# Reordering the head, halving the GpSimd casts and redrawing the instruction lists of a fused sliding-window attention and GEGLU kernel

## The chip, the core and the metric

One core of one Trainium2 chip. The metric is device microseconds of one launch. A profile shows one execution; its span is shorter than the time of the same run (341.0 against 342.76 us before), so spans are compared with spans and times with times. A ratio is the mean time of one kernel's fast runs over that of the other's fast runs of the same rounds, so it is not quite the ratio of the medians quoted.

In the profile PE is TensorE's matmuls, PEld its weight loads, DVE is VectorE, ACT is ScalarE, POOL is GpSimd, SP is SyncE. L581 is line 581 of the kernel; in kernels with halved GpSimd instructions line numbers are 4 higher (L464 is L468, L581 is L585, L427 is L431, L521 is L525).

## The reference

```python
# q, k, v: 8 batches x 8 heads x 576 positions x 64; windows of 32, for heads 4 to 7 dilated by 4
scores = scale * q @ k^T
mask_plain = (rel >= 0) & (rel < 32)
mask_dil   = (rel >= 0) & (rel < 128) & (rel % 4 == 0)
attn = softmax(where(mask, scores, -1e9));  x = attn @ v          # x as 4608 tokens x 512
out = (gelu(x @ w_gate) * (x @ w_val)) @ w_out                    # 512 -> 1536 -> 512
```

## The kernel before

The feed-forward part runs in 8 chunks of 512 tokens. A chunk has a gate stage (192 matmuls of 512 columns, whose results ScalarE puts through gelu and VectorE multiplies) and an output stage (48 matmuls). The attention of later batches is woven between these matmuls, so that TensorE never waits. Where each unit stands is written down in lists of places, one string per stage. A number takes so many feed-forward matmuls; `S` is a pair of heads' score products, `P` the exponential on ScalarE, `M` the mask multiply on VectorE, `D` and `N` the denominators and the products with v, `T` and `B` the reciprocal of the denominators by two VectorE transposes (or `A`, the same by ScalarE), `X` the final product that writes the feed-forward input `xT`. `g` and `u` are the gelu and the product of a gate block, `e` an output copy, `G` and `E` table loads.

```python
    def run_program(c, words, mms, banks):        # walks one list; every engine's instructions are written in this order
        ...
    gates = { ...
        3: ("G 6 e3@2 2 g0 3 u0 2 g1 4 u1 4 g2 ...
    outs = { ...
        3: ("1 u11 5 S16@0 1 E P16 10 e0@3 1 M16 1 S17@0 1 P17 D16@0 N16@1 T16 2 S18@0 M17 ...
```

The head of the program, and what GpSimd does after it:

```python
    warm(20, 7)                                   # 20 matmuls on ones; the granted clock is full from 5.46 us on
    for t in views(1)[2:]:                        # k and v of batch 1: 8 clears (memsets to zero) on VectorE
        zero(t, nc.vector)
    nc.vector.tensor_reduce(class_of, ident..., op=ALU.max)
    biases()                                      # the masks as a bias for batch 0's scores
    for t, hp, eng in ((0, 0, "dve"), (0, 1, "act"), (1, 0, "dve"), (1, 1, "pool")):
        cast_six(eng, t, hp)                      # first q and k rows, fp32 to fp16
    load_w(0); bias_first(0, 4); bias_first(1, 6)
    ...
    def second():
        for t in views(2)[2:4]: zero(t)           # GpSimd
        load_w(2)
        ...                                       # q, k of batch 1, w_out
        for t in views(2)[4:]: zero(t)
        two_masks()
        for t in blocks(vraw[0], 1), blocks(vraw[0], 0): zero(t)
        ...
```

For each later batch, q, k and v come by DMA in fp32, GpSimd casts them to fp16, a DMA transposes q and k, and GpSimd spreads k into block diagonals:

```python
    def cast_plain(t, i):                         # one instruction of 128x1280
        nc.gpsimd.tensor_copy(s16[:, 1280*t : 1280*t+1280]..., st_of(i)...)
    def cast_v(dst, i):                           # two of 64x1152
        for x in range(2): nc.gpsimd.tensor_copy(dst[half, :, half], st[half])
    def spread_plain(kp):                         # two of 64x1152
        for x in range(2): spread(nc.gpsimd, kp..., kdp[:, :, 0:S]..., x)
```

The softmax here doesn't subtract the row's maximum and nothing guards it: scores larger than these inputs give would overflow.

## Time and profile before

| | before |
|---|---|
| median of 4 runs beside the changed kernel | 341.94 us (341.58 to 342.97) |
| span of the profiled run | 341.0 us |
| TensorE, VectorE, ScalarE, GpSimd busy | 97%, 50%, 44%, 40% |
| first score product, first gate matmul | 12.03 us, 21.41 us |
| holes of TensorE after 25 us | 2.23 us in 7 places |

TensorE is the bound, so the question is only where it does not work. "Hole" here is the distance between the starts of two neighbouring matmuls, less what the first one's columns take (216 ns for 512, in proportion for fewer), from the trace's start times. Only holes over 0.11 us are counted, which leaves out the changes between transposes and matmuls of some 0.1 us each. The lines of this profile stand in the prediction.

### The profile page before, as it was taken

To read this page: it belongs to the slowest core of one execution; us is meant where nothing else is said; L and a number is where in the kernel's file an instruction comes from. 1 tells how busy PE (TensorE), PEld (TensorE's weight loads), DVE (VectorE), ACT (ScalarE), POOL (GpSimd) and SP (SyncE) were. 2 spreads that over 40 slices of the span, in tenths; PEclk is the share of its full clock that TensorE was granted. 3 is DMA by queue.
4 is the path that set the end of the run, shared out by engine and by line. 5 is a ranking of instruction groups with operands and counts; after the bars stand their busy time and mean duration, and the time that the engine had idled before them with its cause. 6 is when DMAs were issued, how large, how long until landed. Compare 5 with 4: busy or idle time off the path is not lost.

```text
span 341.0 us, 6228 instructions
## 1 busy us (share of the span) xinstructions
PE 331.2 (97%) x2404; PEld 169.4 (50%) x2404; DVE 171.1 (50%) x265; ACT 150.7 (44%) x222; POOL 135.8 (40%) x194
## 2 busy tenths in 40 slices
PE   7879999999999999999999999999999999999996
PEld 3744456444644465445554465446544544444443
DVE  7864454533843465335983389446833423303320
ACT  2653456635553457335623553346434353223321
POOL 8697777475407556556626701492000000000000
PEclk9999999999999999999999999999999999999999
DMA  7999977997749699898689517981100110020002
GB/s 183 198 194 198 199 164 167 261 188 186 237 117 187 164 222 170 226 232 188 203 209 196 146 63 187 233 191 68 64 0 2 62 63 1 0 94 31 0 31 94
DMA packets 108957, 47.89 MB, mean 140 GB/s; under 512 B 83584, under 2 KB 104448, under 8 KB 108928
## 3 DMA queue, kind: packets, MB, share of 16 engines
q1 hardware_dynamic: 97200, 39.99, 48.3%
q0 software_dynamic: 11184, 6.79, 14.2%
q10 hardware_dynamic: 544, 0.72, 0.8%
q8 instruction: 19, 0.31, 0.4%
q14 instruction: 10, 0.08, 0.1%
HBM read 37.75 MB, written 9.44 MB: 138 GB/s over the span
## 4 chain that ended last, share of the span: by engine, by line
PE 88%; DVE 8%; issue 2%; POOL 1%; ACT 0%; DVEq 0%; ACTq 0%
PE ps L581 54%; PE ps L588 23%; PE ps L523 5%; PE ps L427 3%; DVE xT L573 1%; DVE P L464 1%; DVE dt L543 1%; PE ps L362 1%; DVE rb L560 1%; PE ps L612 1%; DVE v L196 1%; DVE q L196 1%; POOL q L261 1%; DVE dense L345 1%; DVE bias L131 0%
## 5 line engine op out<-in xcount | busy, mean ns | idle before, releaser
L733 DVE SCALAR_TENSOR_TENSOR u_all<-g,ps 128x512 f16<-128x512 f16 x108 | 73.9, 685 | 107.9 <-PE ps L581 100.7
L728 ACT ACTIVATE g<-ps 128x512 f16<-128x512 f32 x108 | 64.3, 597 | 114.1 <-PE ps L581 114.1
L581 PE MATMUL ps<-xT,wg 128*128 128x512 f16 x432 | 112.6, 379 | 0.2
L581 PE MATMUL ps<-xT,wv 128*128 128x512 f16 x432 | 112.5, 379 | 0.0
L588 PE MATMUL ps<-wo,u_all 128*128 128x512 f16 x420 | 101.5, 379 | 0.0
L581 PEld LDWEIGHTS <-wg 128*128 128x128 f16 x432 | 42.1, 98 | 50.3
L581 PEld LDWEIGHTS <-wv 128*128 128x128 f16 x432 | 41.9, 98 | 50.2 <-issue 0.9
L588 PEld LDWEIGHTS <-u_all 128*128 128x128 f16 x420 | 37.5, 97 | 36.8
L261 POOL COPY q<-dense 64x512 f16<-64x512 f16 (+2 forms) x56 | 36.4, 677 | 25.6 <-DMA dense<-s 22.9
L459 ACT ACTIVATE P<-ps 128x832 f16<-128x832 f32 (+1 forms) x32 | 26.7, 836 | 21.9 <-PE ps L427 21.2
L250 POOL CAST v<-stage 64x1152 f16<-64x1152 f32 x28 | 33.0, 1179 | 4.4 <-DMA stage<-in_v_dram 3.4
L599 ACT ACTIVATE osb<-ps 128x512 f32<-128x512 f32 x34 | 20.3, 596 | 32.1 <-PE ps L588 31.6
L573 DVE TENSOR_TENSOR xT<-ps,rb 128x576 f16<-128x576 f32 x32 | 29.6, 928 | 9.4 <-ACT rb L554 4.7
L210 POOL CAST s<-stage 128x1280 f16<-128x1280 f32 x12 | 15.4, 1280 | 46.9 <-DMA stage<-in_q_dram 32.5
L543 DVE STREAM_TRANSPOSE dt<-ps 128x576 f32<-128x576 f32 x21 | 16.3, 774 | 14.5 <-PE ps L523 14.3
L222 POOL CAST s<-stage 128x512 f16<-128x512 f32 x24 | 14.4, 631 | 10.7 <-DMA stage<-in_q_dram 9.0
L523 PEld LDWEIGHTS <-two_ones 128*128 128x128 f16 x176 | 13.5, 97 | 8.3 <-issue 1.7
L523 PE MATMUL ps<-P,two_ones 128*128 128x64 f16 (+8 forms) x176 | 16.2, 226 | 0.8 <-DVE P L464 0.6
L523 PEld LDWEIGHTS <-v 128*128 128x128 f16 x280 | 13.8, 98 | 5.4 <-issue 1.0
L560 DVE STREAM_TRANSPOSE rb<-rc 128x576 f32<-128x576 f32 x21 | 16.2, 769 | 0.2
L464 DVE TENSOR_TENSOR P<-P,two_d 128x768 f16<-128x768 f16 x14 | 10.6, 759 | 9.4 <-ACT P L459 9.4
L427 PEld LDWEIGHTS <-q 128*128 128x128 f16 x252 | 13.0, 98 | 4.5 <-POOL q L261 0.2
(72 smaller groups left out, 174.9 us busy)
## 6 DMA issues: line engine op xcount, KB each, us to landing
out_dram<-osb SPq DMA_DIRECT2D x35, 256.0 KB, 2.2
stage<-in_v_dram SPq DMA_DIRECT2D x32, 144.0 KB, 3.7
stage<-in_v_dram SPq DMA_DIRECT2D x28, 128.0 KB, 3.1
stage<-in_q_dram SPq DMA_DIRECT2D x24, 128.0 KB, 3.0
stage<-in_k_dram SPq DMA_DIRECT2D x24, 128.0 KB, 3.0
stage<-in_q_dram SPq DMA_DIRECT2D x6, 512.0 KB, 5.0
stage<-in_k_dram SPq DMA_DIRECT2D x6, 512.0 KB, 5.8
wg<-in_moe_w_gate_dram POOLq DMA_DIRECT2D x6, 256.0 KB, 6.8
```

The source lines that it names most:

```text
L250: nc.gpsimd.tensor_copy(dst[half, :, half], st[half])
L261: eng.tensor_copy(dst[half, :, :, half], src[half])
L427: nc.tensor.matmul(o, lhs, rhs, start=st, stop=True, skip_group_check=True)
L459: nc.scalar.activation(pt[:, 0 : src.shape[1]], src, AF.Exp, bias=0.0, scale=scale)
L523: nc.tensor.matmul(o, lhs, rhs, start=st, stop=True, skip_group_check=True)
L543: nc.vector.transpose(dt.rearrange("p b c -> p (b c)"), psf[:, c0 : c0 + S])
L573: nc.vector.tensor_tensor(dst, num, rb, ALU.mult)
L581: nc.tensor.matmul(ps[:, bank, :], w[:, kc, ns], xT[kc][:, tok], start=first, stop=end)
L588: nc.tensor.matmul(ps[:, bank, :], u_all[:, fc, tb * P : (tb + 1) * P], wo_t[fc // 4][:, fc % 4, :], start=(fc == 0), stop=(fc == NNB - 1),)
L599: nc.scalar.activation(osb, ps[:, bank, :], AF.Copy, bias=0.0, scale=1.0 / USCALE)
L728: nc.scalar.activation(g, ps[:, gate_banks(c, args[0])[0], :], AF.Gelu)
L733: nc.vector.scalar_tensor_tensor(u_all[:, nb, :], tiles.pop(("g", nb)), USCALE, val, ALU.mult, ALU.mult)
```

## The change

The intent: VectorE makes the bias masks before most of its clears, so that the first casts wait for data alone; GpSimd's long instructions are halved, so that a mask multiply that meets one is held up for less time (the one at 87.80 us took 1.55 us beside a cast of 1.25 us, one of the same shape at 124.03 us 0.49); the lists are drawn up anew with longer VectorE durations, so that a late VectorE instruction does not stop TensorE. With the lists go two smaller edits: the last columns of k (`rest` in the diff) are copied from PSUM on VectorE or ScalarE, for the later batches instead of by GpSimd from a copy, and the order of the first gate matmuls changes. The core of the diff (cut marks are dots):

```diff
     def cast_plain(t, i):
-        nc.gpsimd.tensor_copy(... "p (g k c) -> p k g c" ...)
+        for g in range(2):
+            nc.gpsimd.tensor_copy(s16[:, 1280 * t + 640 * g : 1280 * t + 640 * g + 640]..., st_of(i)...[:, :, g])
...  (cast_v and spread_plain in the same way, two halves by g)
-            copy("pool" if b else "dve", rest, kdd[:, hp, :, P:NCL]...)
+            copy(("dve", "act")[eng], rest, col.rearrange("p (r i) -> p i r", r=8)[:, 64:R8, :])
...
-    for t in views(1)[2:]:
-        zero(t, nc.vector)
     nc.vector.tensor_reduce(class_of, ...)
+    zero(views(1)[2], nc.vector)
     biases()
+    zero(views(1)[3], nc.vector)
...
     def second():
-        for t in views(2)[2:4]:
+        load_w(2)
+        for t in views(1)[4:] + views(2)[2:4]:
             zero(t)
-        load_w(2)
...
         3: (   # gate stage of chunk 3
-            "G 6 e3@2 2 g0 3 u0 2 g1 4 u1 ...
+            "2 e3@2 X15 2 G 6 g0 3 u0 g1 4 u1 ...
         4: (
-            "G 3 T20 1 N20@1 e3@3 2 B20 g0 3 X20 3 u0 1 g1 1 D21@0 N21@1 T21 ...
+            "3 X18 N19@1 e3@3 3 G 1 X19 4 D20@0 1 T20 1 g0 N20@1 2 g1 1 u0 2 u1 3 B20 ...
...  (all lists of gates 1 to 7 and outs 0 to 6 are new, and the order of kc at the start of gates 1 to 4)
```

## The prediction

> **What bounds the kernel now.** I read the page's busy table first, then the waits of TensorE, then the chain that ended last in order of time, then the timelines of the first 25 us and of the stretches where TensorE waits.
>
> The busy table, then TensorE's groups in the page, then the answer on whom TensorE waited for over the whole span:
>
> ```profile
> PE 331.2 (97%) x2404; PEld 169.4 (50%) x2404; DVE 171.1 (50%) x265; ACT 150.7 (44%) x222; POOL 135.8 (40%) x194
> ...
> L581 PE MATMUL ps<-xT,wg 128*128 128x512 f16 x432 | 112.6, 379 | 0.2
> ```
> ```profile
> PE ps L521 <- issue: 1.6, 1, 1.6
> PE ps L628 <- DVE ones L66: 1.5, 1, 1.5
> PE ps L359 <- DVE s L345: 0.9, 1, 0.9
> PE ps L523 <- DVE P L464: 0.6, 1, 0.6
> ...
> PE ps L406 <- DVE bias L141: 0.5, 1, 0.5
> PE ps L521 <- DVE dt L543: 0.4, 1, 0.4
> ```
>
> TensorE is the bound: it is busy 97% of 341.0 us, and the span's other 3% is in the first 25 us and a few short waits. A single matmul is shown as 379 ns, but in the long runs 96 of them take 20.72 us (243.30 to 264.02 in the chain), which is 216 ns from start to start. The row therefore hides any hole shorter than about 160 ns, so I also compared the distance between the starts of neighbouring matmuls with 216 ns (or its share for narrower ones). After 25 us that leaves some 0.7 us that is merely eight changes between transposes and matmuls, and 2.3 us that is waiting: 0.26 at 50.4, 0.76 at 88.4, and 0.07, 0.13, 0.30, 0.12, 0.36, 0.30 between 130 and 171. That 2.3 us and the head are all that a reordering can win; the work of TensorE itself does not change (the order listing has the same 2404 matmuls).
>
> The head, from the timelines of VectorE and TensorE:
>
> ```profile
> 7.25 0.54 DVE L196 MEMSET v<- 64x576 f32 x1 [0.16 <-issue]
> 7.82 0.29 DVE L653 TENSOR_REDUCE class_of<-ident 128x4 f16<-128x128 f16 x1
> ...
> 8.42 1.09 DVE L131 TENSOR_TENSOR bias<-late_of,class_of 64x64 f16<-64x64 f16 x2
> ...
> 9.64 1.02 DVE L345 CAST s<-u_all 96x768 f16<-96x768 f32 x2
> ```
> ```profile
> 8.44 0.87 PE L406 MATMUL ps<-bias,ident 128*128 128x480 f16 x6 [0.50 <-DVE bias L141]
> 10.24 1.19 PE L359 MATMUL ps<-ident,s 96*128 96x96 f16 x24 [0.94 <-DVE s L345]
> ...
> 18.60 0.22 PE L521 MATMUL ps<-P,v 64*64 64x32 f16 x3 [1.62 <-issue]
> ```
>
> Eight clears, 0.70 us from start to start, keep VectorE until 7.8 us; then the bias masks take 1.9 us, and only then come the two casts, though the q rows had landed at 7.56 us and the k rows at 8.32. TensorE's first real work starts at 10.24.
>
> The worst later wait, in VectorE's and GpSimd's timelines:
>
> ```profile
> 87.80 1.55 DVE L464 TENSOR_TENSOR P<-P,two_d 128x768 f16<-128x768 f16 x1
> ```
> ```profile
> 87.69 1.25 POOL L210 CAST s<-stage 128x1280 f16<-128x1280 f32 x1 [2.08 <-DMA stage<-in_k_dram]
> ```
>
> The same mask multiply takes 0.49 us at 124.03. Here it ends at 89.35, which is 0.41 us after GpSimd's cast ends at 88.94: it stood still while that cast ran.
>
> [...] The 28 mask multiplies take 19.3 us together; at the undisturbed 0.49 and 0.53 us (two_d, two_p) they would take 14.3, so about 5 us goes to such blocking. [...] 19 packets of 16 KB in the instruction queue. The first starts at 16.38 and takes 0.96 us, and TensorE stands from 16.98 to 18.60 with nothing released; I read this as a late block. [...] what splitting costs on GpSimd I take from this trace alone.
>
> **The change, part by part.**
>
> 1. Head of VectorE. Four v clears go to GpSimd (4 x 0.70 = 2.8 us), two go behind the bias masks. Then: small clears until 2.3, class_of, two clears to 4.1; the masks then have GpSimd's band (4.07) and late_of (ends 4.34) and take 1.9 us, to about 6.0; two more clears to 7.4. The casts now wait for data: q at 7.56 to 8.1, k at 8.32 to 8.9. TensorE: warm-up to about 7.9, bias products without their 0.50 wait to 8.6, transposes of q at once, of k after ScalarE's and GpSimd's casts (GpSimd's ends at 9.20), done at about 9.6 instead of 11.3. That is 1.7 us, but not all of it stays: the next transposes read the dilated q rows, which land at 10.16 either way. They started at 11.40 and can start at 10.2: **1.2 us** is left. I expect TensorE's first score products at 10.7 to 10.9 instead of 12.03.
>
> 2. Does the block of instructions swallow that? [...] TensorE reaches the gap earlier still, so the stand is longer, but it ends at about 17.4 instead of 18.60. The chain behind it (5.8 us to the steady run at 24.4) has the same instructions. Gain kept: **1.2 us**, between 0.3 and 1.8.
>
> 3. Loads on GpSimd. The third weight load is issued before the clears (from 19.5, not 21.9), the clears grow from 4 to 8 (+2.4 us), so the q and k loads of batch 1 are issued at 27.3 rather than 24.8. The weights ahead of them land only by 32.5, so the DMA queue doesn't run dry; the six q rows still land near 33.6, five us before use. **0.**
>
> 4. Halves on GpSimd. 12 casts of 128x1280, 14 spreads and 28 v casts of 64x1152 become twice as many. Spacing of copies is 1.17 us for 1152 columns and about 0.59 for 512, so 0.13 is fixed: 54 x 0.13 = 7 us more on an engine that is 40% busy, about 1 us per batch, where spreads end 3 us or more before use except for batch 1. For it: its score products move one matmul later, and the end-columns now come from PSUM on VectorE, so two GpSimd copies (1.0 us) and their 1.4 us of waits go; I work out a margin of 0.5 us for the scores and 1 us for its first v product. The longest block on VectorE falls from 1.25 to about 0.7 us. **This alone is worth perhaps 0.5 us**, of the hole at 88.4.
>
> 5. The new lists. One denominator goes from two VectorE transposes to ScalarE; mask multiplies and final products are later relative to their inputs; in batches 4 to 7 parts of the attention move from the output stage into the gate stage. Between 158 and 171 us the chain is nearly all VectorE (its busy time is 9.93 of 10 us from 160 to 170), costing 1.1 us of holes; the new list moves the normalisation of pairs 19 to 21 past it. In the gate stage a u product may be 1.7 us late before TensorE minds (8 matmuls of 216 ns against 0.69), and one transpose (0.77) or product (up to 1.13) between two of them fits. I expect 0.8 of the 2.3 us of holes to stay or come back elsewhere. Parts 4 and 5 together: **1.5 us**.
>
> Sum: 342.15 - 1.2 - 1.5 = **339.4 us**.
>
> **The rivals.**
> (a) The head is hidden by data: weights or the instruction block set the start of the steady run. For it: the DMA queue is full; the block cost 1.6 us. Against: first weights land at 18.44, gates start at 21.4. Then only 1.5 is won: 340.7.
> (b) New waits of TensorE[...]: a v product of batch 1 nine matmuls earlier, or deferred normalisation crowding the u products. For it: VectorE is already at 80 to 100% in stretches. Against: GpSimd has margins and the lists were drawn with longer VectorE times. It would cost 1 to 3 us: 341 to 342.5.
> (c) Everything works and the head also shortens behind the block: up to 1.7 + 2.0 us, 338.0 or a little lower.
>
> **Range and chances.** The sum is 339.4; (c) gives 338.0, (a) with some of (b) 341.1. I give 338.0 to 341.1. Runs before spread 341.72 to 342.97, about 0.4%. Faster by over 2% needs 335.3, beyond all that can be won; slower by over 2% needs 6.8 us of new waits. Chances: 0.01 faster, 0.97 within, 0.02 slower.
>
> **What would show it.** Part 1: casts on VectorE at 7.6 and 8.4, first scores near 10.8. Part 2: the stand of TensorE without a releaser ends near 17.4 and the steady run starts near 23.2; if it still ends at 18.6, (a) holds. Part 3: the weights land by 32.5 as before. Part 4: no mask multiply above about 1.2 us, and spreads of 64x576 at about 0.65. Part 5: no hole over 0.3 us between 158 and 171, and TensorE's waits after 25 us under 1 us. What would make it wrong: a wait of TensorE on GpSimd's spreads or v casts at 44 to 56 us, or on xT at the starts of gate stages.

## The result

| | before | changed |
|---|---|---|
| median | 341.94 us (4 runs) | 339.26 us (4 runs, 338.70 to 339.65) |
| ratio, 95% interval | | 0.9916 (0.9888 to 0.9943) |
| span of the profiled run | 341.0 us | 337.0 us |
| first score product, first gate matmul | 12.03, 21.41 us | 11.10, 19.57 us |
| stand of TensorE in the first v products | 1.80 us, until 18.60 | 0.89 us, until 16.75 |
| holes of TensorE after 25 us | 2.23 us | 0.40 us |
| longest mask multiply | 1.55 us | 1.09 us |

The changed kernel is 0.8% faster; 339.4 had been predicted. The two profiles differ by 4.0 us of span, more than the medians, because the profiled run of before was one of its slower runs and that of the changed kernel its fastest.

The busy table and the whole answer on TensorE's waits, changed kernel:

```profile
PE 330.5 (98%) x2404; PEld 169.4 (50%) x2404; DVE 166.2 (49%) x260; ACT 150.5 (45%) x223; POOL 145.8 (43%) x250
```
```profile
PE ps L632 <- DVE ones L66: 1.5, 1, 1.5
PE ps L525 <- issue: 0.7, 1, 0.7
PE ps L525 <- DVE dt L547: 0.4, 1, 0.4
PE ps L431 <- POOL q L263: 0.2, 1, 0.2
PE ps L431 <- DVE dense L349: 0.2, 1, 0.2
```

The same 2404 matmuls. The waits on the casts (`DVE s`), the bias and the mask multiply (`DVE P`) are gone; the wait without a releaser has fallen from 1.6 to 0.7 us; a new one on GpSimd's spread has come, 0.2 us. The mask multiplies of the changed kernel (minimum, median and longest in ns), and TensorE's timeline at the new wait:

```profile
L468 DVE TENSOR_TENSOR P<-P,two_p x14: 527/606/1086, 45.5 to 234.8; 128x832 f16<-128x832 f16 x14
L468 DVE TENSOR_TENSOR P<-P,two_d x14: 494/558/1026, 50.2 to 237.1; 128x768 f16<-128x768 f16 x14
```
```profile
43.96 0.54 PE L431 MATMUL ps<-q 128*128 128x96 f16 x9 [0.24 <-POOL q L263]
```

The head, from the timelines of VectorE and TensorE of the changed kernel (start, duration, instruction, idle time before it and its releaser):

```profile
4.13 0.47 DVE L141 TENSOR_SCALAR bias<-band 64x96 f16<-64x96 f16 x2 [0.37 <-POOL band L115]
...
7.69 0.61 DVE L349 CAST s<-u_all 96x768 f16<-96x768 f32 x1 [1.10 <-DMA u_all<-in_q_dram]
8.55 0.56 DVE L349 CAST s<-u_all 96x768 f16<-96x768 f32 x1 [0.25 <-DMA u_all<-in_k_dram]
```
```profile
9.32 1.19 PE L363 MATMUL ps<-ident,s 96*128 96x96 f16 x24
...
11.10 0.56 PE L431 MATMUL ps<-q,dense 64*64 64x96 f16 x18 [0.18 <-DVE dense L349]
...
16.75 0.22 PE L525 MATMUL ps<-P,v 64*64 64x32 f16 x3 [0.71 <-issue]
```

The casts, which stood behind clears and masks until 9.64 us, now wait for the DMAs (releaser `DMA u_all`).

### The profile page after: what moved, and what is told of

It is laid out like the page before. It is cut to its first block, busy times and chain, and to the rows that moved or that the text cites.

```text
span 337.0 us, 6263 instructions
## 1 busy us (share of the span) xinstructions
PE 330.5 (98%) x2404; PEld 169.4 (50%) x2404; DVE 166.2 (49%) x260; ACT 150.5 (45%) x223; POOL 145.8 (43%) x250
## 4 chain that ended last, share of the span: by engine, by line
PE 86%; POOL 8%; DMA 4%; SPq 1%; issue 1%; DVE 0%; POOLq 0%
PE ps L585 49%; PE ps L592 27%; PE ps L527 6%; PE ps L431 3%; DMA u_all<-in_q_dram 2%; POOL v L196 2%; DMA stage<-in_v_dram 2%; POOL wv L151 1%; POOL wg L151 1%; PE ps L616 1%; POOL wo L154 1%; POOL q L196 1%; SPq L235 1%; POOL q L263 1%; POOL two_p L327 0%
## 5 line engine op out<-in xcount | busy, mean ns | idle before, releaser
L585 PE MATMUL ps<-xT,wg 128*128 128x512 f16 x432 | 114.4, 379 | 0.1
L592 PE MATMUL ps<-wo,u_all 128*128 128x512 f16 x420 | 100.2, 379 | 0.0
L585 PEld LDWEIGHTS <-wg 128*128 128x128 f16 x432 | 41.3, 98 | 47.3
L263 POOL COPY q<-dense 64x576 f16<-64x576 f16 (+2 forms) x70 | 38.3, 580 | 22.4 <-DMA dense<-s 18.7
L252 POOL CAST v<-stage 64x576 f16<-64x576 f32 x56 | 37.8, 700 | 2.0 <-DMA stage<-in_v_dram 0.6
L211 POOL CAST s<-stage 128x640 f16<-128x640 f32 x24 | 16.6, 720 | 44.0 <-DMA stage<-in_q_dram 27.5
L547 DVE STREAM_TRANSPOSE dt<-ps 128x576 f32<-128x576 f32 x20 | 15.5, 776 | 1.3 <-PE ps L527 1.1
L468 DVE TENSOR_TENSOR P<-P,two_d 128x768 f16<-128x768 f16 x14 | 8.8, 628 | 14.7 <-ACT P L463 14.7
L564 DVE STREAM_TRANSPOSE rb<-rc 128x576 f32<-128x576 f32 x20 | 15.4, 772 | 0.3
L527 PE MATMUL ps<-P,v 128*128 128x96 f16 (+1 forms) x280 | 14.8, 199 | 0.0
```

The lines of the kernel that those rows point to most:

```text
L211: nc.gpsimd.tensor_copy(s16[:, 1280 * t + 640 * g : 1280 * t + 640 * g + 640].rearrange("p (k c) -> p k c", k=5), st_of(i).rearrange("p (k ...
L252: nc.gpsimd.tensor_copy(dst[half, NB2 * g : NB2 * g + NB2, half], st[half, NB2 * g : NB2 * g + NB2])
L263: eng.tensor_copy(dst[half, :, :, half], src[half])
L527: nc.tensor.matmul(o, lhs, rhs, start=st, stop=True, skip_group_check=True)
L547: nc.vector.transpose(dt.rearrange("p b c -> p (b c)"), psf[:, c0 : c0 + S])
L585: nc.tensor.matmul(ps[:, bank, :], w[:, kc, ns], xT[kc][:, tok], start=first, stop=end)
```

## The experiments

Twelve runs, each beside runs of the kernel before on the same chip. Three questions: does the head keep its gain (its rival: data hide it); what of the rest is due to the lists and what to the halves; and what is the stand near 16 us. First the readings of all profiles; "stand" is the longest start-to-start distance near 14 to 20 us, with the time at which TensorE goes on.

| run | median us | ratio to before (95%) | first score | stand | first gate matmul | holes after 25 us | longest M |
|---|---|---|---|---|---|---|---|
| before | 341.94 | | 12.03 | 1.80, to 18.60 | 21.41 | 2.23 | 1.55 |
| e9_before | 342.31 (one run) | | 11.94 | 1.09, to 17.79 | 20.61 | 2.65 | 1.61 |
| changed | 339.26 | 0.9916 (0.9888 to 0.9943) | 11.10 | 0.89, to 16.75 | 19.57 | 0.40 | 1.09 |
| e5_after | 339.28 | 0.9932 (0.9912 to 0.9953) | 11.23 | 1.29, to 17.28 | 20.09 | 0.37 | 1.06 |
| e1_head | 340.75 | 0.9976 (0.9954 to 0.9999) | 10.95 | 1.05, to 16.76 | 19.58 | 2.17 | 1.60 |
| e2_lists | 340.17 | 0.9956 (0.9935 to 0.9977) | 12.07 | 1.76, to 18.59 | 21.41 | 0 | 1.52 |
| e3_halves | 341.95 | 1.0009 (0.9986 to 1.0031) | 12.05 | 2.32, to 19.14 | 22.88 | 0.99 | 0.89 |
| e12_halves_again | 341.55 | 0.9995 (0.9970 to 1.0019) | 11.93 | 1.39, to 18.08 | 20.90 | 1.72 | 1.01 |
| e4_after_whole | 339.99 | 0.9956 (0.9933 to 0.9980) | 10.82 | 1.18, to 16.77 | 19.58 | 1.00 | 1.40 |
| e7_clears | 338.78 | 0.9920 (0.9897 to 0.9943) | 11.27 | 1.53, to 17.56 | 20.37 | 0 | 1.06 |
| e6_warm80 | 340.65 | 0.9969 (0.9945 to 0.9993) | 11.16 | 0.93, to 15.01, and 1.39, to 21.21 | 21.41 | 0 | 1.10 |
| e8_both | 340.73 | 0.9969 (0.9945 to 0.9992) | 10.75 | 1.10, to 15.03, and 1.39, to 21.23 | 21.43 | 0 | 1.07 |
| e10_warm60 | 339.20 | 0.9931 (0.9908 to 0.9953) | 10.58 | 1.81, to 16.01 | 20.28 | 0 | 1.06 |
| e11_warm40 | 339.94 | 0.9941 (0.9917 to 0.9966) | 11.25 | 1.67, to 17.58 | 21.11 | 0 | 1.08 |

All results were correct, and all runs but the single one of e9_before (unknown, being single) were fast ones. The granted clock differs: runs at 0.995 or less were 0.4 to 1.8 us slower than the mean of the same kernel's runs at 0.998 or more. They were 3 of the 6 of e4_after_whole, e6_warm80, e8_both and e11_warm40, 4 of e3_halves, one or two of the others (none of the first four of the changed kernel and of e9_before), and of before one of 11 in the first call and three of 11 in the third.

### The head alone

```diff
 # the kernel before, with the new head and the new order of loads and clears in second()
```

> The kernel before with the new head alone: bias masks ahead of two of the clears, four v clears moved to GpSimd behind the third weight load. Theory (the gain is a head part, a list part and a small part from the halves): the steady run of matmuls starts 1.2 to 1.9 us earlier than the 23.4 of before (changed kernel: 21.5), but up to 0.6 us is lost again between 43 and 51 us, where GpSimd now comes later with the spreads of batch 1 while the lists are the old ones; net 0.8 to 1.6 us faster than before. Rival (the head is hidden by the data): within 0.3 us of before.

It gained 0.8 us by the ratio (0.24% of 342.0; the interval is 0.03 to 1.6 us). The head itself does more: the first gate matmul stands at 19.58 us, not at 21.41 or 20.61. The rest is lost behind it, as TensorE's waits and VectorE's timeline of this run show:

```profile
PE ps L427 <- POOL q L261: 0.5, 1, 0.5
PE ps L521 <- DVE dt L543: 0.4, 1, 0.4
PE ps L523 <- DVE xT L573: 0.4, 1, 0.4
```
```profile
87.36 1.59 DVE L464 TENSOR_TENSOR P<-P,two_p 128x832 f16<-128x832 f16 x1
```

GpSimd has four clears more ahead of the spreads, so TensorE waits there (a hole of 0.71 us at 43.5), and the old lists keep their holes (1.46 us after 80 us). The rival "the head is hidden" falls.

### The lists alone, and the halves alone

```diff
 # e2_lists: the kernel before, with all new lists and the end-columns copied from PSUM
 # e3_halves, e12_halves_again: the kernel before, with cast_plain, cast_v and spread_plain in halves
```

> The kernel before with the new lists of places alone (with the end-columns copied from PSUM, which belong to them), GpSimd instructions whole, old head. Theory: the holes of TensorE between 130 and 171 us (1.2 us) and the 0.26 us at 50 go; the hole of 0.76 us at 88.4 goes too if the lists leave the mask multiply enough time; 1.2 to 2.0 us faster than before. Rival (the halves do it, the lists only follow): under 0.5 us faster, with the hole near 88 us still there.

> The kernel before with the GpSimd casts and spreads in halves alone. Theory: the longest mask multiply falls from 1.55 to at most about 1.2 us, the hole at 88.4 us shrinks by up to 0.6 us, GpSimd is about 8 to 10 us busier, and nothing else changes: 0 to 0.6 us faster than before. Rival (halves are the main cause): 1.2 us or more faster, with the holes from 160 to 171 us gone.

> The halves alone a second time, because four of the first six runs had a granted clock of 0.995 or less. Theory: the runs at a clock of 0.998 or more are 0.5 to 1.3 us faster than before's runs of the same clock (as the smaller sum of holes in its first profile, 1.0 against 2.2 us, says), and the slower ones are those where TensorE's clock fell after the stand. Rival: also at full clock the same as before within 0.3 us.

The lists alone gained 1.5 us. TensorE's waits over this whole run:

```profile
PE ps L521 <- issue: 1.6, 1, 1.6
PE ps L628 <- DVE ones L66: 1.5, 1, 1.5
PE ps L406 <- DVE bias L141: 1.0, 1, 1.0
PE ps L359 <- DVE s L345: 1.0, 1, 1.0
PE ps L521 <- DVE dt L543: 0.4, 1, 0.4
PE ps L427 <- DVE dense L345: 0.2, 1, 0.2
```

All of these lie in the first 21 us; after 25 us there is no hole over 0.11 us at all, though mask multiplies of 1.52 us still occur (GpSimd's instructions are whole). The lists leave the room, and such a multiply no longer reaches TensorE. What the lists, the new source of the end columns and the order of the first gate matmuls do each by itself was not tested.

The halves shorten the longest mask multiply as meant. The two_d mask multiplies, minimum, median and longest in ns, of the kernel before and then of e3_halves:

```profile
L464 DVE TENSOR_TENSOR P<-P,two_d x14: 494/582/1553, 51.8 to 266.5; 128x768 f16<-128x768 f16 x14
```
```profile
L468 DVE TENSOR_TENSOR P<-P,two_d x14: 494/558/894, 53.0 to 266.3; 128x768 f16<-128x768 f16 x14
```

The holes fell to 0.99 and 1.72 us in the two profiles, against 2.23 and 2.65. Yet the times did not follow: ratios of 1.0009 and 0.9995. The first run was inconclusive because of its clock; in the second, the five runs at a clock of 0.998 or more have a mean of 341.3 us, against 341.5 for the eight such runs of before in that call. So my expectation for the second run, 0.5 to 1.3 us, missed: the halves alone are worth 0.2 us there, within noise. Nor do the halves shorten all 28 mask multiplies together by much: 16.7 and 18.6 us in these two profiles, against 19.3 and 19.5 in the two of before. The rival of e2 (the halves do it, the lists only follow) falls.

e3's profile shows what a long stand can do. TensorE's timeline:

```profile
19.14 0.26 PE L525 MATMUL ps<-P,v 64*64 64x32 f16 x3 [2.15 <-issue]
```

By the trace's clock records TensorE's clock was at half from 18.96 to 22.37 us, that is for 3.41 us. From the stand's end at 19.14 to the first gate matmul at 22.88 it took 3.74 us, against 2.81 to 2.82 in the nine other profiles with 20 warm-up matmuls: in this profile the stand cost 0.9 us a second time. In all 14 profiles the clock records change only at whole multiples of 3.41 us from their first change (in before from 5.46 us, where the full clock starts, to 339.96, where it ends with the run: 334.51 us, 98 times 3.413; in the changed kernel from 7.13 to 338.22: 331.09 us, 97 times). The next rows are cut on that grid: the 3.41 us before the clock fell and those at half clock, then the stretch of the kernel before that holds its stand. They give the busy time of TensorE, its weight loads, VectorE, ScalarE and GpSimd; the figure after these is the granted clock:

```profile
15.55:18.96 3.41, 1.45 (x45) 1.24 (x44) 1.41 (x3) 2.72 (x4) 2.91 (x5) 1.00 1.45 197
18.96:22.37 3.41, 3.14 (x54) 2.68 (x54) 2.17 (x4) 2.06 (x3) 3.30 (x6) 0.50 1.43 193
```
```profile
15.70:19.11 3.41, 1.79 (x52) 1.53 (x51) 1.97 (x4) 2.55 (x4) 3.19 (x5) 1.00 1.45 196
```

TensorE was busy for 1.45 of 3.41 us ahead of the fall. With 1.79 us in before, and 1.78 in e10_warm60 (12.84 to 16.25), the clock stayed. In these profiles, then, before the end of the run the clock fell only behind the stand that left TensorE 1.45 us of work in such a stretch; with 1.78 us it stayed. An estimate for the low-clock runs: 3.41 us at half clock lose 1.7 us of full clock, which is 0.005 of a span of 338 us, about what they lack (0.993 to 0.995; two at 0.990 lack twice as much). That a stand is behind them is not shown: no other profile caught a fall before the end of its run.

### The kernel before once more

> The kernel before once more, for a second profile of it. Theory (its holes are chance meetings of VectorE's mask multiplies with GpSimd's reads on a list without slack): the sum of holes after 25 us again lies between 1.2 and 2.5 us, but not all at the same places as in the first profile; the stand at the 17th v product is again 1.6 to 2.4 us. Rival (the holes belong to the list itself): the same seven holes within 0.1 us each.

The holes summed to 2.65 us, a little over the range. Four came back at the same matmul of the list: those at 50 (0.26 us), 132.7 (0.13) and 166.3 (0.12) to the hundredth, that at 170 with 0.27 instead of 0.30. The one of 0.76 at 88.4 did not: that of 0.57 at 90.0 stands 31 matmuls later. Those of 0.30 and 0.36 at 162.2 and 168.6 were gone, and there were new ones at 123.7, 125.9, 129.6 and 165.2 (0.13, 0.26, 0.64 and 0.27). VectorE's timeline here shows again a mask multiply of triple length, here of the two_p kind, as in e1_head:

```profile
88.10 1.61 DVE L464 TENSOR_TENSOR P<-P,two_p 128x832 f16<-128x832 f16 x1
```

So both theory and rival hold in part: four holes, 0.8 us together, belong to the old list, and the larger ones change from profile to profile. This multiply ends 0.45 us after GpSimd's cast of 88.01 to 89.26 us, as in the first profile, so the hole near 88 to 90 is such a chance meeting; for the others that was not traced one by one. The stand was 1.09 us, below what I had expected: it varies from run to run, which is why one pair of profiles must not be used to size it.

### The changed kernel again, and with whole instructions

> The changed kernel itself again, on the same chip and in the same rounds as the parts. 2.3 to 3.2 us faster than before. If the parts are independent, the gains of the three parts alone sum to this within 0.6 us; if the lists need the halves or the head needs the lists, the sum is smaller than this.

2.3 us faster by the ratio, 2.7 by the medians. The gains of the three parts alone, 0.8, 1.5 and -0.3 us (e3_halves; 0.2 from its repeat), sum to 2.0 to 2.5: within the noise the parts add up. Each gain has an interval of about 0.7 us to either side, so an overlap of 1 us would not be seen; the runs at a clock of 0.998 or more alone give 1.1, 1.7 and 0.3, together 3.1, against 2.4.

```diff
 # e4_after_whole: the changed kernel, with cast_plain, cast_v and spread_plain whole as before
```

> The changed kernel with its GpSimd casts and spreads whole again (new head and new lists stay). Theory ([...] the new lists leave slack for it): single mask multiplies reach 1.3 us and more again and all 28 take 19 to 21 us instead of 18.7, GpSimd does 7 to 10 us less, TensorE's holes after 25 us change by under 0.4 us; time within 0.4 us of the changed kernel. Rival (the halves are needed by the lists): 0.6 us or more slower than the changed kernel, with new holes of TensorE on a mask multiply or on xT.

The median is 0.7 us higher than e5_after's, but three of its runs had the lower clock; at a clock of 0.998 or more the means are 339.44 and 339.26 us. The longest mask multiply rose to 1.40 us as expected, but all 28 took 17.6 us, less than the 18.7 with halves instead of the 19 to 21 expected; GpSimd did 6.8 us less than in the first profile of the changed kernel and 7.8 less than in the second. So the sum of the mask multiplies varies between profiles about as much as the halves change it. What differs for TensorE in the profile is one place. TensorE's timeline:

```profile
44.57 0.54 PE L427 MATMUL ps<-q 128*128 128x96 f16 x9 [0.83 <-POOL q L261]
```

The first score products of batch 1 need one head pair's spread. In halves it is done with the third of four instructions of 0.67 us; whole, with the second of two of 1.16. The hole there is 1.00 us instead of 0.37. I had expected a change of holes under 0.4 us; it was 0.6, and not on a mask multiply. In the changed kernel the halves are worth that 0.6 us at this place, by the profile; the times, 0.2 to 0.7 us, are not sharper.

### What the stand near 16 us is

Theory: the stand is a late block of TensorE's instructions. In the profile of before the packets of 16 KB in the instruction queue start 127 matmuls apart on average (14 steps from 44.71 to 306.45 us), with their weight loads 254 instructions; so the stand should belong to a count of instructions. Test: put more instructions ahead of it and see whether the stand moves by just that number.

```diff
-    warm(20, 7)                  # 512 columns each
+    warm(80, 7, P)               # e6_warm80: 80 matmuls of 128 columns, in the changed kernel
 # e8_both the same, e10_warm60 with 60 of 170, e11_warm40 with 40 of 256 columns:
 # these three with the moved clears of the next section as well
```

> The changed kernel with the same warm-up columns cut into 80 matmuls of 128 columns instead of 20 of 512: 120 instructions more on TensorE ahead of the first data, no more columns. Theory (the stand of TensorE near 16 us is a late block of instructions [...]): the first instruction packet starts 2 us or more earlier than the 14 to 14.5 us of the changed kernel, the stand of 0.9 to 1.3 us at the third-last v product is gone or shorter, and the run ends 0.5 to 1.2 us earlier than the changed kernel. Rival (it stands for v rows or for a PSUM window): the stand stays at the same matmul and the time is the same within 0.3 us.

> The changed kernel with the narrow warm-up and the moved clears together. If both theories hold their gains add: 0.8 to 1.6 us faster than the changed kernel, about 337.9 us. If TensorE's earlier start only meets the weights or the batch 1 loads later, it gains under 0.5 us.

> The kernel with moved clears, and the warm-up cut into 60 matmuls of 170 columns: 80 instructions earlier, so that by the count of instructions the first block boundary falls at the bias products of the fourth pair and the second one some 12 matmuls into the gate stage, after its block has landed. Theory: the first stand moves 40 matmuls forward, to about 14.7 us, and no second stand forms; the steady run starts 0.3 to 0.8 us earlier than with the moved clears alone, about 338.2 us. Rival: a second stand over 0.5 us remains (the block lands later than I reckon), and the time is 339 us or more.

> As the run before with 40 matmuls of 256 columns: 40 instructions earlier. The first stand moves 20 matmuls forward, to just before the first v products, about 15 us; no second stand, as its boundary lies some 30 matmuls into the gate stage. Theory: 0.1 to 0.5 us faster than the moved clears alone, about 338.5 us. Rival: no difference, since the packet starts no earlier.

The stand moved. In the list of matmuls its place is behind the 17th v product of the first pair in every kernel with 20 warm-up matmuls. With 40, 60 and 80 of them it lies 20, 40 and 60 matmuls ahead of that: after 15 of the fourth pair's 18 score products, ahead of its bias products, and after 3 of the third pair's 18 score products. TensorE's timelines of e6_warm80 (two places) and e10_warm60:

```profile
15.01 0.46 PE L431 MATMUL ps<-q,dense 64*64 64x96 f16 x15 [0.73 <-issue]
...
21.21 0.27 PE L525 MATMUL ps<-P,v 64*64 64x80 f16 x7 [1.20 <-issue]
```
```profile
16.01 0.49 PE L410 MATMUL ps<-bias,ident 128*128 128x288 f16 x5 [1.63 <-issue]
```

A wait for data or for a PSUM window can't move so. The traces of all 14 profiles say it more sharply: TensorE stops after exactly its 223rd matmul, which is 446 instructions with the weight load of each, and every time it goes on 1.26 to 1.59 us after the first packet of 16 KB of the instruction queue has ended. In e6 and e8 it stops once more 128 matmuls later, that is 256 instructions, and goes on 1.44 and 1.59 us after the second packet. But the expected gain failed, though the first packet did start earlier, at 12.19 us in e6 against 13.95 and 14.51 in the two profiles of the changed kernel: the next boundary came forward too, into the last v products before the gate stage, and the second stand was 1.39 us. In e10 and e11 there was no second stand, but no gain either: the first gate matmul came at 20.28 and 21.11, against 20.37 in the kernel with moved clears and 19.57 and 20.09 in the changed one. The block landed later than I had reckoned (TensorE went on at 16.01 instead of 15.2 in e10; in e11 the packet started at 14.76 us, no earlier than the 14.70 of the kernel with moved clears), and with the stand further forward more of the chain lies behind it: 4.3 us from its end to the first gate matmul in e10, 2.8 us in the changed kernel.

### The clears moved

```diff
     def second():
...
         two_masks()
-        for t in blocks(vraw[0], 1), blocks(vraw[0], 0):
-            zero(t)
...
     def second_v():
         cast_v(views(1)[4], 1)
         cast_v(views(1)[5], 2)
+        for t in blocks(vraw[0], 1), blocks(vraw[0], 0):
+            zero(t)
```

> The changed kernel with four of GpSimd's clears (v of batch 3) moved from ahead of the spreads of batch 1 to behind its v casts. Theory: the spreads start up to 2 us earlier, TensorE's wait of 0.3 us on a spread at 44 us goes, nothing else changes: 0.2 to 0.5 us faster than the changed kernel. Rival: the spreads wait for VectorE's copies anyway, no difference.

The wait is gone. GpSimd's and TensorE's timelines of this run:

```profile
41.41 2.65 POOL L263 COPY q<-dense 64x576 f16<-64x576 f16 x4 [1.45 <-DVE dense L349]
```
```profile
44.46 0.59 PE L431 MATMUL ps<-q 128*128 128x96 f16 x9
```

GpSimd is now idle before the spreads and TensorE is not. The median of 338.78 us is the lowest. It is 0.5 us below e5_after, as expected; at 0.9920 (0.9897 to 0.9943) against 0.9932 (0.9912 to 0.9953) the times alone don't separate the two. The profile shows the wait gone, but not the gain: its stand was 0.24 us longer than e5_after's, and its span, 337.6 us, is not shorter than e5_after's 337.5.

## Why the prediction was right

339.4 us was predicted, 339.26 measured; the range was 338.0 to 341.1. The mechanism held, but that the number is hit within 0.2 us is luck as well: the interval of the ratio, 0.9888 to 0.9943, leaves 1.9 to 3.8 us of gain, and two mis-sized terms lie below. By its own steps:

- **Part 1, the head.** Right in mechanism: the casts on VectorE started at 7.69 and 8.55 (7.6 and 8.4 said), and the first scores at 11.10 instead of 10.7 to 10.9. The dilated q rows landed later (10.39 against 10.16; in e5_after at 10.80, with TensorE waiting 0.4 us for them), and in five profiles of the new head with the old warm-up the first scores came at 10.82 to 11.27.
- **Part 2, the block.** The stand's end was foreseen: 16.75 and 17.28 against "about 17.4", the steady run near 22.6 and 23.1 against 23.2. One clause failed: "the stand is longer". It was 0.89 and 1.29 us, against 1.80 and 1.09 before, because the packet came 1.8 us earlier on average over five profiles of each head, not the 1.2 that I had estimated from the head's gain. (The pair of profiles e9 and e5 alone would have let the clause pass.) The gain of 1.2 us is right when sized over several profiles: the first gate matmul comes at 21.08 on average in four profiles of the old head (e3, with its fallen clock, left out) and at 19.84 in five of the new one, 1.24 us earlier; it follows the stand's end by 2.81 to 2.82 us in all nine, so the chain behind the stand is unchanged, as said. The one pair of profiles would have said 1.84. That the stand is a late block was only a reading in the prediction; the moved stands (20, 40 and 60 matmuls forward) and the packet that ends 1.26 to 1.59 us before TensorE goes on bear it out.
- **Part 3, the loads.** Right: the last of the gate and value weights landed at 32.49 (32.5 said) and the six q rows at 33.65 (33.6).
- **Part 4, the halves.** The longest mask multiply is 1.09 us (at most 1.2 said), a spread 0.67 us (0.65 said). Halving cost GpSimd about 0.16 us of busy time for each added instruction (0.13 said): it rose from 135.8 to 145.8 us, of which four more clears of 0.58 us are 2.3 us and two copies fewer of 0.5 us are -1.0, so that 8.7 us fall to 54 instructions. The runs that change nothing else give 0.15 and 0.18 (8.3 us more in e3_halves, 9.8 in e12_halves_again). Mis-sized: "perhaps 0.5 us, of the hole at 88.4". The lists close that hole without the halves. And "a margin of 0.5 us for the scores" of batch 1 was not there: TensorE was there at 43.72 us and waited 0.24 us for a spread. In before it came there at 45.50; its gates now start 1.84 us earlier in this profile and not 1.2, and GpSimd's clears end only at 41.9. By e4_after_whole it is at this place, not at 88 us, that the halves do their work in the changed kernel.
- **Part 5, the lists.** Mis-sized to the safe side: "0.8 of the 2.3 us of holes to stay"; 0.40 and 0.37 us stayed. No hole over 0.3 us lies between 158 and 171 us; none at all does.
- **Sum.** 1.2 for the head and 1.5 for the rest were said. The profiles show 1.24 and about 2.0 (2.23 and 2.65 down to 0.40 and 0.37); the times show 2.9 us in the first comparison and 2.3 in the second. The difference between 3.2 and these is within the scatter of the runs and isn't resolved.
- **The rivals.** (a), the head hidden by data, fell by e1_head. (b), new waits of 1 to 3 us, did not come at the two places it names; the wait on the spreads at 44 us, named as what would make the prediction wrong, came with 0.24 us. (c), the head shortened behind the block too, has a wrong sum: 1.7 + 2.0 off 342.15 is 338.45, not "338.0 or a little lower", so the low end of the range was not derived. It is about what the profiled run shows (338.70 us, 1.84 us at the first gate matmul); the median lies above it, since the stand differs from run to run.

Still open: what sets how late the block lands (its packet started at 13.9 to 14.7 us in five profiles of the new head and at 15.3 to 16.9 in five of the old one, while TensorE was only some 0.9 us ahead), and why some kernels drew the lower clock in half of their runs.

## What to carry to other kernels

When one engine is busy 97% of the time, measure its holes by the distance between instruction starts, and sum them by place before pricing a change: here the whole stake was about 2.3 us of holes and a head. Slack in a list of places was worth more here than speeding up the instruction that is sometimes late (1.5 us against -0.3 and 0.2), since chance meetings (a multiply of 1.5 instead of 0.5 us) then reach nobody. Look for a stand without a releaser in an instruction-dense stretch (here 180 matmuls, some 35 ns apart, from 9.32 to 15.54 us), and move one thing at a time there: with 60 matmuls more ahead of it TensorE stopped 60 matmuls earlier, and once more, for 1.39 us, 128 matmuls on (e6_warm80).
